# Loading the first 128 columns of x alone, in two halves, with w1 slabs between the other columns, in a dense SiLU kernel

## Chip, cores, metric

One core of one Trainium2 chip. The metric is device time in microseconds (us) for one execution, lower is better. Runs are compared against the kernel before in the same rounds on the same chip.

## The reference

```python
B, S, D, F = 1, 2048, 640, 1728        # all bf16
h   = silu(einsum("bsd,df->bsf", x, w1))
out = einsum("bsf,fd->bsd", h, w2)
```

The kernel's matmuls contract over partitions, so x is needed transposed, with D on partitions. x is worked on in four chunks of 512 rows. Chunks 1 to 3 come through transposing DMAs, hidden behind the first chunk's matmuls. Chunk 0 is wanted at once: it is loaded plainly and transposed on TensorE by matmuls with an identity.

## The kernel before

The parts that matter are the opening loads and TensorE's opening. `FB` is 512, `KF` 4, `TPC` 4, `TA` 2, `DT` 5.

```python
# SyncE
load_x(0)                   # x rows 0-127, all 640 columns, 160 KB
load_slab(0)                # w1 rows 0-127, first 512 columns, 128 KB
for j in range(2, TPC):
    load_x(j)
for d in range(3, DT):
    load_slab(d)
for g, (a, b) in enumerate(G_COLS):         # the rest of w1: G0 480 KB, G1 1040 KB
    sp.dma_start(out=w1_sb[:, :, a:b], in_=w1_v[:, :, a:b]).then_inc(sem_w1g[g], 16)
...
# ScalarE, before its table load
act.dma_start(out=x_sb[:, 1, :], in_=xf[P:2 * P, :]).then_inc(sem_xb[1], 16)
for d in range(1, 3):
    act.dma_start(out=w1_sb[:, d, 0:FB], in_=w1_v[:, d, 0:FB]).then_inc(sem_w1[d], 16)
...
# TensorE
busy(W_FIRST)               # 12 + 15 dummy matmuls to raise the clock
need(sem_id, 2)
busy(W_SECOND)
transpose(0)                # five 128x128 transposes of row block 0, ready for two copies
transpose(1)
for j in range(2):
    for d in range(TA):
        early(d, j, j + 1)  # 4 matmuls: w1 slab d, rows of block j
transpose(2)
early(2, 0, 2)
for d in range(3):
    early(d, 2, 3)
transpose(3)
early(3, 0, 3)
for d in range(4):
    early(d, 3, 4)
early(4, 0, 4)
# then the main loop: 240 matmuls of 512 columns (L310 before, L330 after)
```

ScalarE copies the transposes of slabs 0 and 1 out of PSUM, VectorE those of slabs 2 to 4.

Of the kernel before, what the change touches and what calls it, by code (L numbers as in the profile page):

```python
# [8 lines left out]
def bass_standalone__dense_activation_silu__prompt_kernel(  # L9
# [9 lines left out]
    xf = x.flatten_outer_dims()  # L19
# [3 lines left out]
    P = 128  # L23
# [14 lines left out]
    TA = 2  # L38
    W_FIRST, W_SECOND = 12, 15
    assert TPC == 4 and FB + FQ < F and TA * P <= CH and (DT - TA) * P <= CH  # L40

# [59 lines left out]
    with ExitStack() as es:  # L101
# [19 lines left out]
        sem_xb = [sem(f"sem_xb{j}") for j in range(TPC)]  # L121
# [16 lines left out]

        w1_v = w1.rearrange("(d p) f -> p d f", p=P)
        w2_v = w2[0:NF * P, :].rearrange("(f p) d -> p f d", p=P)  # L140
        ones = nc.const_aps.tensor(1.0, [P, CH], bf16)

# [13 lines left out]
        def on_sync(sp):  # L156
            def load_x(j):
                sp.dma_start(
                    out=x_sb[:, j, :], in_=xf[j * P:(j + 1) * P, :]
                ).then_inc(sem_xb[j], 16)  # L160
# [6 lines left out]
            load_x(0)  # L167
            load_slab(0)
            for j in range(2, TPC):
                load_x(j)  # L170
            for d in range(3, DT):
                load_slab(d)
# [42 lines left out]
        def on_tensor(pe):  # L215
# [17 lines left out]
            def transpose(j):  # L233
                need(sem_xb[j], 16)
                if j >= 2:
                    need(sem_cpa, j - 1)
                    need(sem_cpv, j - 1)
                ba = 4 + 2 * (j % 2)
                for d in range(DT):
                    k = d if d < TA else d - TA  # L240
                    ins = pe.matmul(  # L241
                        ps[:, ba + (d >= TA), k * P:(k + 1) * P],
                        lhsT=x_sb[:, j, d * P:(d + 1) * P],
                        rhs=ident[:, :],
                        start=True,
                        stop=True,
                    )
                    if d == TA - 1:
                        ins.then_inc(sem_tpa, 1)
                ins.then_inc(sem_tpv, 1)  # L250

            def early(d, j0, j1):
                need(sem_w1[d], 16)
                need(sem_cpa if d < TA else sem_cpv, j1)
                for f in range(KF):
                    ins = pe.matmul(  # L256
                        ps[:, f, j0 * P:j1 * P],
                        lhsT=w1_sb[:, d, f * P:(f + 1) * P],
                        rhs=xT[:, d, j0 * P:j1 * P],
                        start=(d == 0 and j0 == 0),  # L260
# [3 lines left out]
                    if d == DT - 1 and j1 == TPC:  # L264
                        ins.then_inc(sem_pe1, 1)
# [4 lines left out]
            transpose(0)  # L270
            transpose(1)
            for j in range(2):
                for d in range(TA):
                    early(d, j, j + 1)
            transpose(2)
            early(2, 0, 2)
            for d in range(3):
                early(d, 2, 3)
            transpose(3)
            early(3, 0, 3)  # L280
            for d in range(4):
                early(d, 3, 4)
            early(4, 0, 4)

            for i in range(KF, NU):
# [7 lines left out]
                if i < NB:  # L293
                    need(sem_cpa, TPC)
                    need(sem_cpv, TPC)
# [58 lines left out]
        def on_scalar(act):  # L354
            act.dma_start(
                out=x_sb[:, 1, :], in_=xf[P:2 * P, :]
            ).then_inc(sem_xb[1], 16)
            for d in range(1, 3):
                act.dma_start(
                    out=w1_sb[:, d, 0:FB], in_=w1_v[:, d, 0:FB]  # L360
                ).then_inc(sem_w1[d], 16)
# [3 lines left out]
            for j in range(TPC):  # L365
                act.wait_ge(sem_tpa, j + 1)
                act.copy(  # L367
                    out=xT[:, 0:TA, j * P:(j + 1) * P],
                    in_=ps[:, 4 + 2 * (j % 2), 0:TA * P].rearrange("p (d s) -> p d s", s=P),
# [19 lines left out]
        def on_vector(dve):  # L389
            for j in range(TPC):  # L390
                dve.wait_ge(sem_tpv, j + 1)
# [44 lines left out]
```

## Time and profile before

| | before |
|---|---|
| median of the first 3 runs | 126.31 us (126.29 to 127.24) |
| profiled execution | 126.98 us, span 125.7 us |
| PE busy | 122.9 us, 98% of the span |
| main loop (L310) starts | 10.40 us |

"Span" is the profile's first to last instruction, about 1.3 us shorter than the time. A line of the timeline gives start, length, engine, source line, operation, output<-input, shape and count, and in brackets idle time before it with what ended it. The profile's lines are in the prediction below.

### The profile page before, as it was taken

The numbers are of one execution on the slowest core, as the hardware profiler recorded it, in microseconds if no ns is written. First come the engines' busy times: TensorE is split into PE (matmuls) and PEld (weight loads), VectorE is DVE, ScalarE is ACT, GpSimd is POOL, SyncE is SP. The second block draws the span as 40 slices with busy tenths as digits, with TensorE's granted clock in tenths as the row PEclk, the third lists the DMA queues.
The fourth block names the chain that finished last, engine by engine and source line by source line (L and its number), as shares of the span: only waits on it lengthen the run. The fifth ranks groups of instructions, "written<-read, shape, count | busy, mean of one in ns | idle before, by whom it ended". The sixth has DMA issues, their size and how long they took to land.

```text
span 125.7 us, 1483 instructions
## 1 busy us (share of the span) xinstructions
PE 122.9 (98%) x657; PEld 59.6 (47%) x657; DVE 12.2 (10%) x20; ACT 37.1 (30%) x65; POOL 0.7 (1%) x6
## 2 busy tenths in 40 slices
PE   7999999999999999999999999999999999999994
PEld 7884444444444444444444444443444443444452
DVE  0330000000000000000000000000700003920421
ACT  3328555555555555555540000001500000000000
POOL 2000000000000000000000000000000000000000
DMA  3992999990000000000000000000346000731022
GB/s 101 357 390 80 218 204 203 310 390 28 0 0 0 0 3 0 0 0 5 0 0 0 0 0 0 0 0 5 75 92 219 0 0 0 258 110 54 0 104 94
DMA packets 17014, 10.37 MB, mean 82 GB/s; under 512 B 10736, under 2 KB 17008, under 8 KB 17008
## 3 DMA queue, kind: packets, MB, share of 16 engines
q1 hardware_dynamic: 16432, 9.82, 26.4%
q10 hardware_dynamic: 576, 0.46, 1.1%
q8 instruction: 5, 0.08, 0.3%
q14 instruction: 1, 0.01, 0.0%
HBM read 5.16 MB, written 2.62 MB: 62 GB/s over the span
## 4 chain that ended last, share of the span: by engine, by line
PE 95%; DMA 2%; ACT 0%; issue 0%
PE ps L344 47%; PE ps L310 41%; PE ps L256 4%; DMA x_sb<-in_x_dram 2%; PE ps L301 2%; PE ps L241 1%; ACT o_sb L381 0%
## 5 line engine op out<-in xcount | busy, mean ns | idle before, releaser
L310 PE MATMUL ps<-xT,w_sb 128*128 128x512 bf16 x240 | 52.0, 379 | 0.0
L344 PE MATMUL ps<-w_sb,hT 128*128 128x512 bf16 (+2 forms) x221 | 45.6, 367 | 0.0
L374 ACT ACTIVATE hT<-ps 128x512 bf16<-128x512 f32 x52 | 30.6, 598 | 24.0 <-PE ps L310 22.4
L310 PEld LDWEIGHTS ps<-xT,w_sb 128*128 128x128 bf16 x240 | 23.5, 98 | 28.3
L344 PEld LDWEIGHTS ps<-w_sb,hT 128*128 128x128 bf16 x221 | 20.9, 98 | 24.5 <-issue 0.6
L399 DVE CAST o_sb<-ps 128x512 bf16<-128x512 f32 (+1 forms) x16 | 10.0, 677 | 104.9 <-PE ps L344 104.9
L344 PE MATMUL ps<-hT,w_sb 128*128 128x512 bf16 x52 | 11.4, 379 | 0.0
L381 ACT CAST o_sb<-ps 128x128 bf16<-128x128 f32 x1 | 0.3, 266 | 34.2 <-PE ps L344 34.2
L381 ACT CAST oT<-ps 128x512 bf16<-128x512 f32 x4 | 2.1, 600 | 22.3 <-PE ps L344 22.3
L344 PEld LDWEIGHTS ps<-hT,w_sb 128*128 128x128 bf16 x52 | 5.0, 98 | 6.3 <-issue 0.4
L256 PE MATMUL ps<-xT,w_sb 128*128 128x128 bf16 (+3 forms) x56 | 5.4, 258 | 0.0
L256 PEld LDWEIGHTS ps<-xT,w_sb 128*128 128x128 bf16 x56 | 4.1, 108 | 0.7
L225 PE MATMUL ps<-const-bfloat16-1.0 128*128 128x128 bf16 x27 | 3.0, 312 | 0.8 <-PEq L421 0.8
L225 PEld LDWEIGHTS ps<-const-bfloat16-1.0 128*128 128x128 bf16 x27 | 2.8, 148 | 0.7 <-issue 0.7
L392 DVE CAST xT<-ps 128x384 bf16<-128x384 f32 x4 | 2.2, 558 | 6.5 <-PE ps L241 6.5
L367 ACT CAST xT<-ps 128x256 bf16<-128x256 f32 x4 | 1.5, 373 | 3.3 <-PE ps L241 3.3
L301 PE MATMUL ps<-xT,w_sb 128*64 128x512 bf16 x20 | 2.3, 381 | 0.0
L344 PE MATMUL ps<-w_sb,hTl 64*128 64x512 bf16 (+2 forms) x17 | 2.2, 366 | 0.0
L241 PE MATMUL ps<-ident,x_sb 128*128 128x128 bf16 x20 | 2.1, 265 | 0.1
L362 ACT ACT_TABLE_LOAD x1 | 1.3, 1283 | 2.2 <-issue 2.2
L241 PEld LDWEIGHTS ps<-ident,x_sb 128*128 128x128 bf16 x20 | 1.6, 120 | 0.3 <-DMA x_sb<-in_x_dram 0.3
L301 PEld LDWEIGHTS ps<-xT,w_sb 128*64 128x64 bf16 x20 | 1.0, 110 | 1.2 <-ACT hT L374 0.4
(11 smaller groups left out, 3.7 us busy)
## 6 DMA issues: line engine op xcount, KB each, us to landing
out_dram<-o_sb SPq DMA_DIRECT2D x15, 160.0 KB, 1.8
w_sb<-in_w_dram SPq DMA_DIRECT2D x1, 1120.0 KB, 7.6
w_sb<-in_w_dram SPq DMA_DIRECT2D x1, 1040.0 KB, 6.8
w_sb<-in_w_dram SPq DMA_DIRECT2D x1, 960.0 KB, 5.3
x_sb<-in_x_dram SPq DMA_DIRECT2D x3, 160.0 KB, 4.0
w_sb<-in_w_dram SPq DMA_DIRECT2D x1, 480.0 KB, 4.7
w_sb<-in_w_dram SPq DMA_DIRECT2D x3, 128.0 KB, 3.7
w_sb<-in_w_dram ACTq DMA_DIRECT2D x2, 128.0 KB, 3.8
```

The lines of the kernel that those rows point to most:

```text
L225: pe.matmul(ps[:, KF - 1, 0:P], lhsT=ones[:, 0:P], rhs=ones[:, 0:P], start=True, stop=True,)
L241: ins = pe.matmul(ps[:, ba + (d >= TA), k * P:(k + 1) * P], lhsT=x_sb[:, j, d * P:(d + 1) * P], rhs=ident[:, :], start=True, stop=True,)
L256: ins = pe.matmul(ps[:, f, j0 * P:j1 * P], lhsT=w1_sb[:, d, f * P:(f + 1) * P], rhs=xT[:, d, j0 * P:j1 * P], start=(d == 0 and j0 == 0), s ...
L301: ins = pe.matmul(ps[h * FL:(h + 1) * FL, b, :], lhsT=w1_sb[:, d, NF * P:F], rhs=xT[:, d, (c + h) * CH:(c + h + 1) * CH], start=(d == 0), ...
L310: ins = pe.matmul(ps[:, b, :], lhsT=w1_sb[:, d, f * P:(f + 1) * P], rhs=xT[:, d, c * CH:(c + 1) * CH], start=(d == 0), stop=(d == DT - 1),)
L344: ins = pe.matmul(ps[:, bank, 0:width], lhsT=w_op if kind == "T" else h_op, rhs=h_op if kind == "T" else w_op, start=(first2[key] == i), s ...
L362: act.activation(out=warm_sb[:, :], in_=nc.const_aps.tensor(0.0, [P, 1], fp32), func=ACT.Silu)
L367: act.copy(out=xT[:, 0:TA, j * P:(j + 1) * P], in_=ps[:, 4 + 2 * (j % 2), 0:TA * P].rearrange("p (d s) -> p d s", s=P),).then_inc(sem_cpa, 1)
L374: act.activation(out=dst, in_=ps[:, i % NB, :], func=ACT.Silu).then_inc(sem_act1, 1)
L381: act.copy(out=dst, in_=ps[:, place[key], 0:dst.shape[-1]]).then_inc(sem_evb, 1)
L392: dve.tensor_copy(out=xT[:, TA:DT, j * P:(j + 1) * P], in_=ps[:, 5 + 2 * (j % 2), 0:(DT - TA) * P].rearrange("p (d s) -> p d s", s=P),).th ...
L399: dve.tensor_copy(out=o_sb[:, key[1], cols], in_=ps[:, place[key], cols]).then_inc(sem_eva, 1)
```

## The change

The intent: let TensorE start its real work sooner. Instead of waiting for a whole row block of x (160 KB), it waits for two loads of 64 KB that hold only columns 0 to 127 of all 512 rows, enough for the first slab of w1. The other 512 columns follow in two halves of 256 rows, with the slabs of w1 between them, in the order of need. (A slab is 128 rows of w1, first 512 columns; G0 and G1 are the rest of w1.) The dummy matmuls go from 27 to 21. The copies of the transposes are cut anew as well: pieces of 128 or 256 columns, taken in turn by ScalarE and VectorE.

```diff
-    W_FIRST, W_SECOND = 12, 15
+    W_FIRST, W_SECOND = 12, 9
...
+            def load_half(k):
+                js = slice(k * JH, (k + 1) * JH)
                 sp.dma_start(
-                    out=x_sb[:, j, :], in_=xf[j * P:(j + 1) * P, :]
-                ).then_inc(sem_xb[j], 16)
+                    out=x_sb[:, js, P:D], in_=x_v[:, js, P:D]
+                ).then_inc(sem_xh[k], 16)
...
-            load_x(0)
+            sp.dma_start(
+                out=x_sb[:, 0:JH, 0:P], in_=x_v[:, 0:JH, 0:P]
+            ).then_inc(sem_xf[0], 16)
             load_slab(0)
-            for j in range(2, TPC):
-                load_x(j)
-            for d in range(3, DT):
-                load_slab(d)
+            load_half(0)
+            load_slab(1)
+            load_slab(2)
+            load_half(1)
+            load_slab(3)
+            load_slab(4)
...
             act.dma_start(
-                out=x_sb[:, 1, :], in_=xf[P:2 * P, :]
-            ).then_inc(sem_xb[1], 16)
-            for d in range(1, 3):
-                act.dma_start(
-                    out=w1_sb[:, d, 0:FB], in_=w1_v[:, d, 0:FB]
-                ).then_inc(sem_w1[d], 16)
+                out=x_sb[:, JH:TPC, 0:P], in_=x_v[:, JH:TPC, 0:P]
+            ).then_inc(sem_xf[1], 16)
...
+            for i in range(TPC):
+                transpose(i)                        # slab 0, all 512 rows
+            for j in range(TPC - 1):
+                early(0, j * P, (j + 1) * P)
+            transpose(at[1, 0]); transpose(at[2, 0])     # (joined here)
+            early(0, CH - P, CH)
+            transpose(at[3, 0]); transpose(at[4, 0])
+            early(1, 0, HC)
+            early(2, 0, HC, range(KF // 2))
+            transpose(at[1, HC]); transpose(at[2, HC])   # first use of the second half
+            early(2, 0, HC, range(KF // 2, KF))
+            transpose(at[3, HC]); transpose(at[4, HC])
+            early(1, HC, CH)
+            early(2, HC, CH)
+            early(3, 0, CH)
+            early(4, 0, CH)
```

More of the change, by code (lines that the diff above doesn't have):

```diff
@@ L37, in bass_standalone__dense_activation_silu__prompt_kernel @@
     TPC = CH // P
-    TA = 2
-    W_FIRST, W_SECOND = 12, 15
-    assert TPC == 4 and FB + FQ < F and TA * P <= CH and (DT - TA) * P <= CH
+    HC = CH // 2
+    JH = TPC // 2
+    W_FIRST, W_SECOND = 12, 9
+    assert TPC == 4 and FB + FQ < F and DT == 5
     units = [(c, f) for c in range(NC) for f in range(NF)]
@@ L120, in bass_standalone__dense_activation_silu__prompt_kernel @@
         sem_id = sem("sem_id")
-        sem_xb = [sem(f"sem_xb{j}") for j in range(TPC)]
+        sem_xf = [sem(f"sem_xf{k}") for k in range(2)]
+        sem_xh = [sem(f"sem_xh{k}") for k in range(2)]
         sem_tpa = sem("sem_tpa")
@@ L137, in bass_standalone__dense_activation_silu__prompt_kernel @@
         sem_ol = sem("sem_ol")
+        x_v = xf[0:CH, :].rearrange("(j p) d -> p j d", p=P)
         w1_v = w1.rearrange("(d p) f -> p d f", p=P)
@@ L141, in bass_standalone__dense_activation_silu__prompt_kernel @@
         ones = nc.const_aps.tensor(1.0, [P, CH], bf16)
+        turns = [(0, j * P, (j + 1) * P, KF + j) for j in range(TPC)]
+        for k in range(2):
+            turns += [(d, k * HC, (k + 1) * HC, KF + d - 1) for d in range(1, DT)]
+        at = {(d, a): i for i, (d, a, b, bank) in enumerate(turns)}
         def on_gpsimd(pool):
@@ L156, in on_sync @@
         def on_sync(sp):
-            def load_x(j):
+            def load_half(k):
+                js = slice(k * JH, (k + 1) * JH)
                 sp.dma_start(
-                    out=x_sb[:, j, :], in_=xf[j * P:(j + 1) * P, :]
-                ).then_inc(sem_xb[j], 16)
+                    out=x_sb[:, js, P:D], in_=x_v[:, js, P:D]
+                ).then_inc(sem_xh[k], 16)
             def load_slab(d):
@@ L231, in busy, with copied, transpose @@
                     )
-            def transpose(j):
-                need(sem_xb[j], 16)
-                if j >= 2:
-                    need(sem_cpa, j - 1)
-                    need(sem_cpv, j - 1)
-                ba = 4 + 2 * (j % 2)
-                for d in range(DT):
-                    k = d if d < TA else d - TA
+            def copied(i):
+                need(sem_cpv if i % 2 else sem_cpa, i // 2 + 1)
+            def transpose(i):
+                d, a, b, bank = turns[i]
+                need((sem_xh if d else sem_xf)[a // HC], 16)
+                if i >= TPC:
+                    copied(i - TPC)
+                for off in range(0, b - a, P):
                     ins = pe.matmul(
-                        ps[:, ba + (d >= TA), k * P:(k + 1) * P],
-                        lhsT=x_sb[:, j, d * P:(d + 1) * P],
+                        ps[:, bank, off:off + P],
+                        lhsT=x_sb[:, (a + off) // P, d * P:(d + 1) * P],
                         rhs=ident[:, :],
@@ L247, in transpose, with early @@
                     )
-                    if d == TA - 1:
-                        ins.then_inc(sem_tpa, 1)
-                ins.then_inc(sem_tpv, 1)
-            def early(d, j0, j1):
+                ins.then_inc(sem_tpv if i % 2 else sem_tpa, 1)
+            def early(d, a, b, fs=range(KF)):
                 need(sem_w1[d], 16)
-                need(sem_cpa if d < TA else sem_cpv, j1)
-                for f in range(KF):
+                step = HC if d else P
+                for c0 in range(a, b, step):
+                    copied(at[d, c0])
+                for f in fs:
                     ins = pe.matmul(
-                        ps[:, f, j0 * P:j1 * P],
+                        ps[:, f, a:b],
                         lhsT=w1_sb[:, d, f * P:(f + 1) * P],
-                        rhs=xT[:, d, j0 * P:j1 * P],
-                        start=(d == 0 and j0 == 0),
+                        rhs=xT[:, d, a:b],
+                        start=(d == 0 and a == 0),
                         stop=(d == DT - 1),
@@ L263, in early @@
                     )
-                    if d == DT - 1 and j1 == TPC:
+                    if d == DT - 1:
                         ins.then_inc(sem_pe1, 1)
@@ L269, in on_tensor @@
             busy(W_SECOND)
-            transpose(0)
-            transpose(1)
-            for j in range(2):
-                for d in range(TA):
-                    early(d, j, j + 1)
-            transpose(2)
-            early(2, 0, 2)
-            for d in range(3):
-                early(d, 2, 3)
-            transpose(3)
-            early(3, 0, 3)
-            for d in range(4):
-                early(d, 3, 4)
-            early(4, 0, 4)
+            for i in range(TPC):
+                transpose(i)
+            for j in range(TPC - 1):
+                early(0, j * P, (j + 1) * P)
+            transpose(at[1, 0])
+            transpose(at[2, 0])
+            early(0, CH - P, CH)
+            transpose(at[3, 0])
+            transpose(at[4, 0])
+            early(1, 0, HC)
+            early(2, 0, HC, range(KF // 2))
+            transpose(at[1, HC])
+            transpose(at[2, HC])
+            early(2, 0, HC, range(KF // 2, KF))
+            transpose(at[3, HC])
+            transpose(at[4, HC])
+            early(1, HC, CH)
+            early(2, HC, CH)
+            early(3, 0, CH)
+            early(4, 0, CH)
             for i in range(KF, NU):
@@ L293, in on_tensor @@
                 if i < NB:
-                    need(sem_cpa, TPC)
-                    need(sem_cpv, TPC)
+                    copied(len(turns) - 2)
+                    copied(len(turns) - 1)
                 else:
@@ L364, in on_scalar @@
             )
-            for j in range(TPC):
-                act.wait_ge(sem_tpa, j + 1)
+            for n, (d, a, b, bank) in enumerate(turns[0::2]):
+                act.wait_ge(sem_tpa, n + 1)
                 act.copy(
-                    out=xT[:, 0:TA, j * P:(j + 1) * P],
-                    in_=ps[:, 4 + 2 * (j % 2), 0:TA * P].rearrange("p (d s) -> p d s", s=P),
+                    out=xT[:, d, a:b], in_=ps[:, bank, 0:b - a]
                 ).then_inc(sem_cpa, 1)
@@ L389, in on_vector @@
         def on_vector(dve):
-            for j in range(TPC):
-                dve.wait_ge(sem_tpv, j + 1)
+            for n, (d, a, b, bank) in enumerate(turns[1::2]):
+                dve.wait_ge(sem_tpv, n + 1)
                 dve.tensor_copy(
-                    out=xT[:, TA:DT, j * P:(j + 1) * P],
-                    in_=ps[:, 5 + 2 * (j % 2), 0:(DT - TA) * P].rearrange("p (d s) -> p d s", s=P),
+                    out=xT[:, d, a:b], in_=ps[:, bank, 0:b - a]
                 ).then_inc(sem_cpv, 1)
```

## The prediction

> **What bounds the kernel now.** I read the page's chain first, then the timeline from 3 to 11 us, then the waits, then stretches of half a microsecond for the DMA.
>
> The chain that ended last (us from the start, us long, what):
>
> ```profile
> PE 95%; DMA 2%; ACT 0%; issue 0%
> ...
> 0.74 3.09 DMA x_sb<-in_x_dram
> 3.83 0.05 issue
> 3.88 1.25 PE ps L241 x10
> 5.12 1.33 PE ps L256 x16
> 6.46 0.28 PE ps L241 x5
> 6.74 1.14 PE ps L256 x16
> 7.88 0.28 PE ps L241 x5
> 8.16 2.41 PE ps L256 x24
> 10.56 51.80 PE ps L310 x240
> ```
>
> One DMA, the first 128 rows of x, holds TensorE until 3.88; from there TensorE alone carries the program to its end. 240 matmuls of L310 in 51.80 us are 215.8 ns each for 512 columns. The change touches nothing behind L310's first matmul, so its whole worth is how much earlier that matmul starts. The timeline has it at 10.40 (the chain counts ends of pipelined matmuls, so it says 10.56).
>
> The timeline of the opening, PE and copies (start, us, what):
>
> ```profile
> 0.78 3.04 PE L225 MATMUL ps<-const-bfloat16-1.0 128*128 128x128 bf16 x27 [0.78 <-PEq L421]
> ...
> 3.87 0.99 PEld L241 LDWEIGHTS ps<-ident,x_sb 128*128 128x128 bf16 x10 [0.32 <-DMA x_sb<-in_x_dram]
> 3.88 1.25 PE L241 MATMUL ps<-ident,x_sb 128*128 128x128 bf16 x10
> 4.31 0.37 ACT L367 CAST xT<-ps 128x256 bf16<-128x256 f32 x1 [0.65 <-PE ps L241]
> ...
> 4.92 1.54 PE L256 MATMUL ps<-xT,w_sb 128*128 128x128 bf16 x16
> 6.24 0.32 PEld L241 LDWEIGHTS ps<-ident,x_sb 128*128 128x128 bf16 x5
> 6.30 0.44 PE L241 MATMUL ps<-ident,x_sb 128*128 128x128 bf16 x5
> ...
> 6.58 1.30 PE L256 MATMUL ps<-xT,w_sb 128*128 128x256 bf16 x16
> ```
>
> Three things are to be seen. The 27 dummy matmuls are over just before x comes. From 3.88 no PE or PEld line carries a wait for data, so the old order of transposes and early matmuls already hides every later load. And TensorE changes speed: ten transposes take 4.92 - 3.88 = 1.04 us (104 ns each), the next five 6.58 - 6.30 = 0.28 us (56 ns each). The sixteen L256 matmuls between take 6.30 - 4.92 = 1.38 us; with n of them at 107 and the rest at 56 ns, n is 9.5, so the switch lies near 5.9 us. The PEclk column says 1.00 throughout and hides it.
>
> **The opening as a sum.** 20 transposes of 128 columns, and 44 x 128 + 4 x (256 + 384 + 512) columns of L256, are 12,800 columns in 76 matmuls. At full speed 12,800 / 2.4 = 5.33 us; the 20 or so matmuls before 5.9 are 2,560 columns at half speed, 1.07 us more; 56 fast matmuls at 2.5 ns overhead are 0.14. The sum is 6.54 us; the timeline has 10.40 - 3.88 = 6.52. So there is no bubble in it to remove, and the 128-column matmuls cost nothing special.
>
> **What the Trainium skill says.** "TensorE: Matmul & The Clock Gate", section "Back-to-back issue gap": N / 1.2 ns cold and N / 2.4 + 2.5 ns warm, 107 and 56 ns for 128 columns. The trace agrees (104 and 56). The same page, "What's actually happening": the clock is released after a busy window of about 3.4 us, and the window is free-running. One trace cannot show whether it runs free, but 5.9 is 5.1 us after the first dummy matmul, which would fit one partly filled window and then a full one. "DMA: Bandwidth & Descriptors", section "Issuing engines are not separate DMA queues": loads from both queues share the same 16 engines. The trace agrees as far as it goes: the total stays between 329 and 409 GB/s from 2.5 to 9.5 us, with two queues in use or one. Its "Specifications" give 512 B as the least transfer for line rate. The new first loads move rows of 256 B; nothing in this trace's opening does, so their cost is not shown here.
>
> **Part 1, the first loads.** Before, TensorE waits for 160 KB beside 160 KB from the other queue. After, two loads of 64 KB stand first. From the stretches (the last column is GB/s):
>
> ```profile
> 1.50:2.00 0.50, 0.50 (x7) 0.50 (x6) 0.00 (x0) 0.00 (x0) 0.00 (x0) 1.00 0.50 61
> 2.00:2.50 0.50, 0.50 (x8) 0.50 (x6) 0.00 (x0) 0.34 (x1) 0.00 (x0) 1.00 0.70 131
> 2.50:3.00 0.50, 0.50 (x8) 0.50 (x6) 0.00 (x0) 0.50 (x1) 0.00 (x0) 1.00 0.94 329
> 3.00:3.50 0.50, 0.50 (x7) 0.50 (x6) 0.00 (x0) 0.49 (x2) 0.00 (x0) 1.00 1.08 380
> ```
>
> 30, 65, 165 and 190 KB arrive in these halves: 95 by 2.5, 260 by 3.0, 450 by 3.5. The two old x loads, 320 KB, are through by about 3.16; the queue views have them landed at 0.74 + 3.1 = 3.83 and 0.74 + 3.3 = 4.05, so 0.7 to 0.9 us later. The same lag on 128 KB (through by 2.6) gives 3.3 to 3.5. The short rows may eat a little, a smaller load may be told sooner; the author's cut from 27 to 21 dummies ends them near 0.84 + 20 x 0.107 + 0.1 = 3.1, which suggests 3.1 to 3.3 was aimed at. I take a start at 3.35, half a microsecond earlier.
>
> **Part 2, the later loads.** By the same byte curve and lag I place slab 0 (256 KB in all) at 3.8, the first half of the other columns (512) at 4.5, slabs 1 and 2 at 4.9 and 5.3, the second half (1,024) at 6.1, slabs 3 and 4 at 6.4 and 6.8, the next weight group at about 8. All issue from one queue at 0.47 us each (the old one's spacing), the last of these eight at about 4.0: well ahead of their landing, so issuing does not bind.
>
> **Part 3, TensorE's new order.** The columns are the same 12,800: 20 x 128 of transposes, then 16 x 128 + 16 x 256 + 8 x 512. 60 matmuls instead of 76 save 16 x 2.5 ns = 0.04 us. What is new is a thin start: only four transposes (3.35 to about 3.75) before the first matmul that needs a copy. A copy began 0.35 us after the start of the slow matmul it waited for (3.96 to 4.31); ScalarE takes 0.27 us for 128x128 (row L381). So 3.35 + 0.35 + 0.27 + 0.07 (my guess for the signal) = 4.04: a bubble of 0.3 us. Then twelve matmuls to 5.32, four transposes to 5.75, and part of the next group until the clock rises at 5.9. Slow columns done by then: 4 x 128 + (5.90 - 4.04) x 1,200 = 2,744, against 2,560 before. The rest, 10,056 columns, is 4.19 us plus 0.1 of overhead: 10.19, or **0.21 us** earlier.
>
> The half microsecond of start shrinks to this because the bubble eats 0.3 of it, and because what is gained before 5.9 is gained at half speed.
>
> Against it one wait: the transpose of the second half's slab 1 is issued near 6.92; its second matmul at 6.98 plus 0.26 (6.35 to 6.61 in the trace) starts ScalarE's 0.37 us copy, ready at 7.68 with the signal, where TensorE would be at about 7.58. **0.1 us** back. The copies split evenly otherwise, and the old ones of 0.56 us on VectorE become ones of some 0.3 and 0.4. The page's ScalarE and VectorE are idle enough here. Sum: 10.40 - 0.21 + 0.10 = 10.29, some 0.1 us saved. If x lands at 3.2 instead, another 0.07.
>
> **Rivals.** *A load takes over as the wait.* The last halves and slabs stand in one queue; if the 256 B rows slow the first loads by 0.5 us, everything behind moves too. But the margins are wide: the second half is due at 6.1 and wanted at 6.9, slab 3 at 6.4 and wanted near 8.5. Only x's first half and slab 0 have none; 0.5 us there costs 0.25 us net: 126.5. *The clock rises later.* Two gaps, 3.1 to 3.35 and 3.75 to 4.04, against one of 0.3 now, fall into the stretch before 5.9. If that is too idle and the rise comes one window (3.4 us) later, the cold time costs 3.4 / 2 = 1.7 us: 128. For it: 0.5 to 0.6 us idle in a window where 0.3 passed. Against: TensorE still works over 80% of it. I give it one in ten. *No bubble, all the gain.* If the copies come sooner than I think, 0.5 us of early start gives 0.25 plus 0.04: about 126.0. *The clock rises earlier* has no reason in the change.
>
> **Range and chances.** The time before is 126.31, with one run of three at 127.24, so single runs move by nearly 1 us by themselves. I predict 126.2 and take 125.6 to 127.0: the lower end holds the full gain and some luck, the upper a late load or a median from the slower kind of run. A change of 2% needs 2.5 us. The whole wait for x is 3.1 us and most of it stays, so faster by that is all but excluded (0.01). Slower needs the late clock and more besides, 1.7 not being enough (0.02). Within 2%: 0.97.
>
> **What would show it.** Right: the first transpose at 3.2 to 3.4; a PE or PEld idle of about 0.3 us before the first L-line of early matmuls, put down to a ScalarE copy; cadence from 107 to 56 ns near 5.9; no DMA wait on TensorE after slab 0; L310's successor starting at 10.2 to 10.4; everything behind it the same length. Wrong: a first transpose not before 3.7 (small rows), or TensorE waiting for a slab or a half, or the change of cadence at another time, which would outweigh all the rest: every microsecond by which it moves is half a microsecond of the total.

## The result

127.43 us median (127.31 to 127.58, 6 runs) against 126.58 (126.29 to 127.24, 6 runs). The ratio is 1.0061, interval [1.0033, 1.009]. A ratio is the mean time of one kernel's runs over that of the other's in the same rounds, so not quite the ratio of the medians. Executions over 1.5% slower than the fastest of the same kernel are left out of the means. So the change is 0.6% slower: within 2%, as given most of the chance, but above the range of 125.6 to 127.0 and in the other direction than the small gain that was foretold. 0.3 us of the miss on the absolute number is the baseline, whose median rose from 126.31 to 126.58 with three more runs.

The chain that ended last, after the change (start, us, what):

```profile
0.74 0.45 SPq L176
...
2.74 0.43 SPq L172
3.17 0.04 issue
3.22 4.26 DMA x_sb<-in_x_dram
7.48 0.05 issue
7.53 0.40 PE ps L255 x4
...
11.05 51.80 PE ps L330 x240
```

Before, the chain left the DMAs at 3.83 us and stayed on TensorE. Now it leaves them at 7.48: SyncE's issues one after another, then a load issued at 3.22 that takes 4.26 us to land. It is the second half of x. L330's 51.80 us are those of L310 to the hundredth, so nothing behind it has changed.

The timeline of TensorE's opening after the change:

```profile
3.03 0.61 PE L255 MATMUL ps<-ident,x_sb 128*128 128x128 bf16 x4
3.35 0.48 ACT L383 CAST xT<-ps 128x128 bf16<-128x128 f32 x2 [0.61 <-PE ps L255]
...
3.73 1.20 PEld L270 LDWEIGHTS ps<-xT,w_sb 128*128 128x128 bf16 x12 [0.36 <-DMA w_sb<-in_w_dram]
3.76 1.44 PE L270 MATMUL ps<-xT,w_sb 128*128 128x128 bf16 x12
...
6.28 0.91 PE L270 MATMUL ps<-xT,w_sb 128*128 128x256 bf16 x6
...
7.52 0.23 PEld L255 LDWEIGHTS ps<-ident,x_sb 128*128 128x128 bf16 x4 [0.62 <-DMA x_sb<-in_x_dram]
...
10.89 2.32 PE L330 MATMUL ps<-xT,w_sb 128*128 128x512 bf16 x10
```

The first transpose is at 3.03, sooner than hoped. There is the small bubble before 3.76. But then TensorE stands idle until 7.52 for the second half, and the main loop starts at 10.89 instead of 10.40: 0.49 us, which is the spans' difference (126.14 - 125.66). The rise of the clock, from half speed to full, is read from the distance of starts: of the six matmuls from 6.28 the first takes 0.196 us to the next, the others 0.109, and at half speed it would be 0.21. So some (0.196 - 0.109) x 2 = 0.17 us of it were at half speed, and the clock rose near 6.45, not at 5.9. (The same working gives 5.93 for the kernel before.)

Landings of the opening loads, us from the start (issue plus time to landing, per load):

| | before | after | before, second trace | after, second trace |
|---|---|---|---|---|
| first x | 3.83 and 4.03 | 2.98 and 3.17 | 3.45 and 3.68 | 2.97 and 3.16 |
| slab 0 | 4.33 | 3.60 | 4.04 | 3.47 |
| slab 1, slab 2 | 4.56, 5.87 | 5.29, 6.40 | 4.26, 6.39 | 5.41, 6.71 |
| rest of x | 5.64 and 6.10 | 4.96 and 7.48 | 6.18 and 6.70 | 5.07 and 7.49 |
| slab 3, slab 4 | 6.46, 6.79 | 7.85, 8.93 | 7.05, 7.39 | 7.83, 8.16 |
| G0, G1 | 8.24, 10.89 | 10.28, 12.89 | 8.67, 11.67 | 10.60, 13.24 |

(The second traces were taken later, see the experiments.)

The bytes are the same, but after the first x and slab 0 nearly everything is late, in the end by 2 us (against the second trace before, by less). Where it is lost can be read from half-microsecond stretches. The columns are the busy time and count of PE, PEld, DVE, ACT and POOL, then granted clock, busy share of the DMA engines and GB/s. Before:

```profile
4.50:5.00 0.50, 0.50 (x7) 0.50 (x6) 0.37 (x1) 0.34 (x2) 0.00 (x0) 1.00 1.03 330
5.00:5.50 0.50, 0.50 (x8) 0.50 (x6) 0.50 (x2) 0.21 (x1) 0.00 (x0) 1.00 1.06 361
5.50:6.00 0.50, 0.50 (x8) 0.50 (x6) 0.22 (x1) 0.00 (x0) 0.00 (x0) 1.00 1.09 378
```

After:

```profile
4.50:5.00 0.50, 0.50 (x7) 0.44 (x5) 0.00 (x0) 0.00 (x0) 0.00 (x0) 1.00 0.79 182
5.00:5.50 0.50, 0.50 (x7) 0.49 (x6) 0.00 (x0) 0.05 (x1) 0.00 (x0) 1.00 0.71 152
5.50:6.00 0.50, 0.50 (x8) 0.50 (x6) 0.33 (x1) 0.33 (x1) 0.00 (x0) 1.00 0.65 184
```

Half the rate, with the DMA engines idle for a fifth to a third of the time, although eight loads on SyncE's queue had been issued by 4.6 us. Another dip, of 133 GB/s, lies at 3.0 to 3.5. The second trace of the kernel before has a dip of its own, shallower and shorter (233 and 255 GB/s from 4 to 5 us, then 359 and 369), for which nothing waits; that after has 268, 115 and 166 in the three stretches. Single packets, the pieces in which a DMA engine moves a load, go the same way, but less clearly: of those read between 2.5 and 9 us, 48 and 45 took over 130 ns ("long" below) in the two traces after (up to 1,260 ns), 13 and 24 in the two before (up to 1,540 ns). The usual packet of 1,024 B takes 46 ns in both.

### The profile page after: what moved, and what is told of

It is laid out like the page before. It is cut to its first block, busy times and chain, and to the rows that moved or that the text cites. A ratio compares the mean times of both kernels' runs of the same rounds, so it can differ in the third digit from the quotient of the medians.

```text
span 126.1 us, 1445 instructions
## 1 busy us (share of the span) xinstructions
PE 123.0 (98%) x635; PEld 58.9 (47%) x635; DVE 12.2 (10%) x22; ACT 37.6 (30%) x67; POOL 0.7 (1%) x6
## 4 chain that ended last, share of the span: by engine, by line
PE 93%; DMA 3%; SPq 2%; issue 0%; ACT 0%
PE ps L364 47%; PE ps L330 41%; DMA x_sb<-in_x_dram 3%; PE ps L270 2%; PE ps L321 2%; SPq L172 1%; PE ps L255 0%; SPq L176 0%; SPq L167 0%; ACT o_sb L396 0%
## 5 line engine op out<-in xcount | busy, mean ns | idle before, releaser
L330 PE MATMUL ps<-xT,w_sb 128*128 128x512 bf16 x240 | 52.0, 379 | 0.0
L330 PEld LDWEIGHTS ps<-xT,w_sb 128*128 128x128 bf16 x240 | 23.5, 98 | 28.3
L270 PE MATMUL ps<-xT,w_sb 128*128 128x128 bf16 (+2 forms) x40 | 6.1, 312 | 0.1
L238 PE MATMUL ps<-const-bfloat16-1.0 128*128 128x128 bf16 x21 | 2.4, 309 | 0.8 <-PEq L435 0.8
L383 ACT CAST xT<-ps 128x256 bf16<-128x256 f32 (+1 forms) x6 | 2.0, 337 | 3.9 <-PE ps L255 3.9
L255 PE MATMUL ps<-ident,x_sb 128*128 128x128 bf16 x20 | 2.6, 274 | 0.3 <-DMA x_sb<-in_x_dram 0.3
L407 DVE CAST xT<-ps 128x256 bf16<-128x256 f32 (+1 forms) x6 | 2.2, 380 | 6.6 <-PE ps L255 6.6
L238 PEld LDWEIGHTS ps<-const-bfloat16-1.0 128*128 128x128 bf16 x21 | 2.2, 143 | 0.7 <-issue 0.7
```

Of the source, the lines that this page charges most:

```text
L238: pe.matmul(ps[:, KF - 1, 0:P], lhsT=ones[:, 0:P], rhs=ones[:, 0:P], start=True, stop=True,)
L255: ins = pe.matmul(ps[:, bank, off:off + P], lhsT=x_sb[:, (a + off) // P, d * P:(d + 1) * P], rhs=ident[:, :], start=True, stop=True,)
L270: ins = pe.matmul(ps[:, f, a:b], lhsT=w1_sb[:, d, f * P:(f + 1) * P], rhs=xT[:, d, a:b], start=(d == 0 and a == 0), stop=(d == DT - 1), sk ...
L330: ins = pe.matmul(ps[:, b, :], lhsT=w1_sb[:, d, f * P:(f + 1) * P], rhs=xT[:, d, c * CH:(c + 1) * CH], start=(d == 0), stop=(d == DT - 1),)
L383: act.copy(out=xT[:, d, a:b], in_=ps[:, bank, 0:b - a]).then_inc(sem_cpa, 1)
L407: dve.tensor_copy(out=xT[:, d, a:b], in_=ps[:, bank, 0:b - a]).then_inc(sem_cpv, 1)
```

## The experiments

Theories at the start: the **one queue** (all loads but one now issue from SyncE), the **form** of the new loads (pieces of 1,024 B out of rows of 1,280, two row blocks per load), and the mere **place** of the second half in the line. Variants of the changed kernel first, run on one chip (kernel before there: 126.88 median).

**Row blocks.**

```diff
-                sp.dma_start(
-                    out=x_sb[:, js, P:D], in_=x_v[:, js, P:D]
-                ).then_inc(sem_xh[k], 16)
+                for j in range(k * JH, (k + 1) * JH):
+                    sp.dma_start(
+                        out=x_sb[:, j, P:D], in_=x_v[:, j, P:D]
+                    ).then_inc(sem_xh[k], 16)
```

> The changed kernel, but each half of x's other columns comes as two loads of 128 rows instead of one load of 256 (two row blocks per partition); 2 more DMAs on SyncE's queue, each some 0.47 us of issue. In the changed kernel the second half lands at 7.48 us and TensorE starts L330 at 10.89. If the two-block form of the load is what makes it slow: second half at 6.5 or before, the wait of 0.51 us gone, 126.9 us or less. If the one queue is at fault (fewer loads in flight at once): no better, the second half at 7.5 or later (two more loads), 127.4 to 127.8 us. If only its place in the queue: 7.5, 127.4.

Measured: 127.28 us (126.83 to 127.7), ratio 1.0047 [1.0013, 1.008]. The second half landed at 6.77 and TensorE no longer waited for it. That alone would speak for the form. But the slow stretches had only moved: 180 GB/s at 4.5 to 5.0, 295 and 307 up to 6.0, and then 164 and 202 from 6.5 to 7.5, G0 landed at 10.19 (10.28 in the changed kernel), and L330 waited for it. Neither forecast held (6.5 and 126.9 for the form, 7.5 and 127.4 to 127.8 for the queue): a mixed verdict, against the number of loads in its simplest reading too, as two more loads did not make the whole slower.

**Whole rows.**

```diff
-                    out=x_sb[:, js, P:D], in_=x_v[:, js, P:D]
+                    out=x_full[:, js, :], in_=x_v[:, js, :]
...
-                        lhsT=x_sb[:, (a + off) // P, d * P:(d + 1) * P],
+                        lhsT=(x_full if d else x_sb)[:, (a + off) // P, d * P:(d + 1) * P],
```

> The changed kernel, but the halves are loaded as whole rows of 1280 B (all 640 columns, into a buffer of their own), so that what is read in DRAM is contiguous again; a quarter more bytes in them. If the pieces of 1024 B out of 1280 B rows stall the DMA engines: the long packets (over 130 ns) from 3.0 to 5.6 us become few as before, the second half lands at 6.6 or sooner in spite of 128 KB more, 127.0 us or less. If the single queue or the place in it is at fault: at 7.5 to 7.9, 127.4 to 127.7 us.

Measured: 127.78 us (127.74 to 127.99), ratio 1.0078. 49 long packets, the second half at 7.75: late with whole rows too, so the broken rows are not needed for it. That they add nothing is not shown. The stretches from 4.5 to 6 us were less low here (319, 228 and 281 GB/s), slab 0 came late instead (4.71), and TensorE waited 1.2 us for it, which is part of the time.

**Two queues.**

```diff
             load_half(0)
-            load_slab(1)
-            load_slab(2)
             load_half(1)
...
+            for d in range(1, 3):            # on ScalarE's queue
+                act.dma_start(
+                    out=w1_sb[:, d, 0:FB], in_=w1_v[:, d, 0:FB]
+                ).then_inc(sem_w1[d], 16)
```

> The changed kernel, but slabs 1 and 2 are issued from ScalarE's queue right after its first load of x, as the kernel before does; order on SyncE's queue otherwise as it is. If one queue alone is what starves the DMA engines (they moved 150 to 180 GB/s from 4.5 to 6 us where the kernel before had 330 to 378): that stretch is back over 300 GB/s, the second half lands at 6.3 or sooner, the wait of 0.51 us is gone and the time is 126.4 to 126.9 us. If the form of the halves' loads is at fault: bytes stay slow, the second half at 7 or later, 127.2 us or more. Both can be told apart by the GB/s from 4.5 to 6.

The stretches of this variant:

```profile
4.50:5.00 0.50, 0.50 (x8) 0.50 (x6) 0.00 (x0) 0.00 (x0) 0.00 (x0) 1.00 0.95 320
5.00:5.50 0.50, 0.46 (x5) 0.24 (x3) 0.00 (x0) 0.00 (x0) 0.00 (x0) 1.00 1.07 361
5.50:6.00 0.50, 0.30 (x6) 0.30 (x7) 0.00 (x0) 0.00 (x0) 0.00 (x0) 1.00 1.10 365
```

The rate is that of the kernel before, long packets are down to 24, the second half lands at 6.22 and G0 at 8.26. So moving two loads cures the rate, with the form of the halves as it was. The time was not cured: 128.01 us median (127.04 to 129.15), two of four runs near 127.1 and two near 129 (one of them counted slow, its span 127.8). In the trace, of a good run, the first half now lands at 5.66 instead of 4.96, as slabs 1 and 2 now come beside it, and TensorE idles twice, 3.4 to 4.07 and 5.3 to 5.70. The first gap ends with ScalarE's first copy, not with a load: two issues more on ScalarE put its table load off from 1.25 to 2.27 us and that copy from 3.35 to 3.67. The expected 126.4 to 126.9 was missed. The bad runs were not traced; what they may be came out later.

**Half first.**

```diff
             load_half(0)
+            load_half(1)
             load_slab(1)
             load_slab(2)
-            load_half(1)
```

> The changed kernel with the second half of x ahead of slabs 1 and 2 in the queue. If only its place in the queue is at fault: the half lands some 0.9 us sooner (6.5), slabs 1 and 2 0.9 later (6.2 and 7.2), and as slab 1 is wanted at 6.28 and slab 2 at about 6.7, the wait moves to slab 2 and shrinks a little: 127.2 us. If a low rate of bytes is the cause, whoever stands third in line waits: about the same time, 127.2 to 127.6 us, with TensorE waiting for w1 instead of x.

Measured: 127.3 us (126.99 to 127.35), ratio 1.0032 [1.0006, 1.0058]. The second half at 5.66, slabs 1 and 2 at 6.06 and 6.79, and TensorE waits three times for w1, 1.0 us in all on its weight loads. Whoever stands third in the line waits, as the low rate would have it; another place cures nothing by itself. Whether it helps a little is open (the interval overlaps the changed kernel's).

**The old kernel on one queue**, on another chip (kernel before there: 127.14 median). This asks whether one queue slows the old loads as well.

```diff
             load_x(0)
+            load_x(1)
-            load_slab(0)
+            for d in range(3):
+                load_slab(d)
...
-            act.dma_start(out=x_sb[:, 1, :], ...)
-            for d in range(1, 3):
-                act.dma_start(out=w1_sb[:, d, 0:FB], ...)
```

> The kernel before with its nine first loads all issued by SyncE, in about the order of their issue before (x0, x1, slabs 0 to 2, x2, x3, slabs 3 and 4); shapes of the loads and TensorE's order untouched. If one queue alone lowers the rate, whatever the shape of the loads: under 250 GB/s in some of the stretches from 3 to 6.5 us where the kernel before had 330 to 378, many long packets, slab 4 landing after 7.5 instead of 6.79, TensorE waiting for w1 or x for some 0.3 to 1 us, 127.2 us or more. If it takes the new shapes (256 B rows, two-block halves) as well: the rate stays over 320 from 3.5 us on, slab 4 before 7.3, 126.3 to 127.1 us.

Its stretches:

```profile
4.50:5.00 0.50, 0.50 (x8) 0.47 (x6) 0.50 (x2) 0.37 (x1) 0.00 (x0) 1.00 0.92 305
5.00:5.50 0.50, 0.50 (x9) 0.44 (x8) 0.47 (x1) 0.00 (x0) 0.00 (x0) 1.00 0.84 214
5.50:6.00 0.50, 0.50 (x10) 0.34 (x7) 0.00 (x0) 0.00 (x0) 0.00 (x0) 1.00 0.66 161
```

127.38 us (127.36 to 127.75), ratio 1.0045 [1.0002, 1.0087]; 53 long packets; slab 4 at 7.85; TensorE waits 0.6 us for x. All marks set for one queue were met (under 250 GB/s, slab 4 after 7.5, a wait of 0.3 to 1 us, 127.2 us or more). None of the change's new shapes is in this kernel, and it shows the changed kernel's dip.

**Both kernels once more**, for second traces.

> The kernel before, unchanged, for a second trace. Theory: the clock's rise comes at another moment in each execution (5.9 us in the first trace, 5.2 to 6.3 in the traces of the variants), and the kernel before, which waits for no load after the first, follows it by half: with the rise at another time t, L310 starts near 10.40 - (5.93 - t) / 2. Rival: the rise is fixed by the kernel's own matmuls, then it lies at 5.9 again and the spread of the times comes from elsewhere.

The kernel before: the clock rose near 6.04, L310 started at 10.34, the dummies ended at 3.61 and x had landed at 3.45, 0.4 us sooner than in the first trace. Half of the 0.27 us earlier start less half of the 0.11 later rise is 0.08 us, against 0.06 found. So the rise and the start of work both count by half, but the rise had hardly moved: that it wanders between executions of this kernel is not shown, and the forecast from the rise alone, 10.46, missed. What did differ between the two traces is the loads (table and dip above).

> The changed kernel, unchanged, for a second trace. Theory: its opening is set by the landing of the second half of x, not by the clock, which is why its six times lie within 0.27 us where those of the kernel before spread over 0.95. So with the rise of the clock elsewhere than 6.3 us, the second half lands at 7.3 to 7.6 again and L330 starts at 10.7 to 11.0 all the same, the wait for the half being longer when the clock rises sooner. Rival (the late rise of 6.33 in the first trace made the time): a rise at 5.3 would bring L330 to 10.4.

The changed kernel: second half at 7.49, L330 at 10.89, both as in the first trace. The rise was at 6.45, as in the first, so this run did not tell the two theories apart as meant. The times do so better: seven runs of the changed kernel lie within 0.27 us, while most variants that do not wait for the second half spread by 0.7 to 2.1 us (half first, which waits for w1 instead, by 0.36).

**Halves on ScalarE's queue**, the same chip.

```diff
-            load_half(0)  ... load_slab(4)
+            for d in range(1, DT):
+                load_slab(d)
...
+            for k in range(2):               # on ScalarE's queue
+                js = slice(k * JH, (k + 1) * JH)
+                act.dma_start(
+                    out=x_sb[:, js, P:D], in_=x_v[:, js, P:D]
+                ).then_inc(sem_xh[k], 16)
```

> The changed kernel with both halves of x issued from ScalarE's queue and all slabs from SyncE's: two queues again, the first half earlier than in the two-queue variant before (landing 5.66 there). By equal shares: slab 0 at 3.9, first half and slab 1 at 4.7, slab 2 at 5.3, second half and slab 3 at 6.3, slab 4 at 6.7. If the rate of the queues is what set the changed kernel's time: no wait for a load but that for slab 0, L330 at 10.1 to 10.3 with the clock's rise at 5.9 and sooner when it rises sooner, 126.3 to 126.8 us, level with or a little under the kernel before on the same chip. If the two-block halves are slow by themselves: the second half after 7, 127.2 us or more. Some executions may miss a window of the clock, TensorE idling some 0.5 us before slab 0, and come out 1.7 us longer.

The loads were cured (363 to 383 GB/s from 4.5 to 6, second half at 6.33) except for slab 0, which landed at 4.68. The time, forecast at 126.3 to 126.8, was by far the worst: 128.76 us (128.38 to 129.06), ratio 1.0142. Its timeline says why:

```profile
4.72 1.46 PE L260 MATMUL ps<-xT,w_sb 128*128 128x128 bf16 x12 [1.13 <-DMA w_sb<-in_w_dram]
...
7.26 1.49 PE L260 MATMUL ps<-xT,w_sb 128*128 128x256 bf16 x6
...
9.39 0.44 PE L245 MATMUL ps<-ident,x_sb 128*128 128x128 bf16 x4
...
12.27 1.03 PE L320 MATMUL ps<-xT,w_sb 128*128 128x512 bf16 x4
```

The six matmuls from 7.26 take 0.21 us each, half speed. The rise comes only at 9.5, 3.3 us later than in the next variant (6.2), about the window of 3.4 us that the prediction took from the Trainium skill ("TensorE: Matmul & The Clock Gate", "What's actually happening"). This is the prediction's second rival. Only one run was traced; the other three times lie close to its 128.85.

**The same with eleven dummy matmuls in the idle time**, and three more, on a third chip (kernel before there: 126.86 median).

```diff
             for i in range(TPC):
                 transpose(i)
+            busy(11)
```

> The variant with both halves on ScalarE's queue (its clock rose only at 9.5 us, after TensorE had idled from 3.4 to 4.7 for slab 0; 128.76 us) with eleven dummy matmuls put into that idle time. All loads and real instructions are the same. If the idle time is what made the clock miss its window: rise at 6.4 or before, L320 at 10.5 to 11.0 instead of 12.27, 126.9 to 127.4 us. If the late rise came from something else: no change, 128.4 to 129 us.

```profile
3.42 1.38 PE L228 MATMUL ps<-const-bfloat16-1.0 128*128 128x128 bf16 x11
...
6.16 0.43 PE L245 MATMUL ps<-ident,x_sb 128*128 128x128 bf16 x4
...
7.03 0.82 PE L260 MATMUL ps<-xT,w_sb 128*128 128x256 bf16 x6
...
11.03 2.32 PE L321 MATMUL ps<-xT,w_sb 128*128 128x512 bf16 x10
```

127.39 us (126.88 to 127.61), ratio 1.0033. Slab 0 was as late as without them (4.86), but the clock rose at 6.2 and the main loop started at 11.03 instead of 12.27. Idle time in the opening thus costs more than itself: work that computes nothing won 1.2 us. This also fits the two bad runs of the two-queue variant, though those were not traced.

**Fewer, larger loads on the one queue.**

```diff
-            load_half(0)  ... load_slab(4)
+            sp.dma_start(
+                out=x_sb[:, :, P:D], in_=x_v[:, :, P:D]
+            ).then_inc(sem_xh[0], 16)
+            for d in (1, 3):
+                sp.dma_start(
+                    out=w1_sb[:, d:d + 2, 0:FB], in_=w1_v[:, d:d + 2, 0:FB]
+                ).then_inc(sem_w1[d], 16)
```

> The changed kernel on its one queue, but with fewer and larger loads after slab 0: both halves of x as one load (512 KB), slabs 1 and 2 as one, slabs 3 and 4 as one (256 KB each). What in the one queue is slow? If it is the number of loads behind each other (each load's end holds the queue up): the stretches from 4.5 to 6.5 us come back over 300 GB/s and the long packets fall from 45 to 30 or less. If it is one queue's reads as such, whatever their grouping: 150 to 250 GB/s in some stretches and 45 or more long packets again. The time says little here, as the coarse loads land late for TensorE: x's other columns at 5.5 to 6, 127 to 128 us.

```profile
4.50:5.00 0.50, 0.27 (x5) 0.09 (x2) 0.00 (x0) 0.00 (x0) 0.00 (x0) 1.00 1.07 379
5.00:5.50 0.50, 0.00 (x0) 0.00 (x0) 0.00 (x0) 0.00 (x0) 0.00 (x0) 1.00 1.10 377
5.50:6.00 0.50, 0.00 (x0) 0.00 (x0) 0.00 (x0) 0.00 (x0) 0.00 (x0) 1.00 1.13 369
```

Still one queue, and the full rate. G0 landed at 8.78. The long packets fell to 34, between the two marks (30 or fewer, 45 or more). The dip from 3 to 4 us stayed (121 and 129 GB/s), where the first x, slab 0 and the large load still follow each other. The time, 127.86 us (127.46 to 129.69, the last counted slow, at a granted clock of 0.987), ratio 1.0066, goes with the coarse load of x, for which TensorE waited 1.3 us, as expected. So it is not one queue as such, but many small loads one behind another in it.

**No wait for the second half** (wrong result).

```diff
-                need((sem_xh if d else sem_xf)[a // HC], 16)
+                need(sem_xh[0] if d else sem_xf[a // HC], 16)
...
-                        lhsT=x_sb[:, (a + off) // P, d * P:(d + 1) * P],
+                        lhsT=x_sb[:, (a + off) // P % (JH if d else TPC), d * P:(d + 1) * P],
```

> The changed kernel with all loads as they are, but the transposes of the second half's columns 128 to 639 read the first half once more, so that nothing waits for the second half of x: a wrong result on purpose, to price that one wait. In the changed kernel the wait is 0.51 to 0.6 us and sets the end. Theory: L330 starts at 10.3 to 10.4 with the clock's rise at 6.3 to 6.4 (and sooner with a sooner rise), 126.8 to 127.0 us, spread again as before. Rival (another load, slab 3 or 4, landing at 7.85 and 8.2 to 8.9, takes its place): wait for w1 and 127.2 us or more.

```profile
10.69 2.55 PE L330 MATMUL ps<-xT,w_sb 128*128 128x512 bf16 x11 [0.21 <-DMA w_sb<-in_w_dram]
```

127.08 us (126.72 to 128.22), ratio 1.003 [0.9983, 1.0077]. Without that wait L330 could have gone at 10.32; it waited until 10.69 for G0, which landed at 10.65. Of 0.57 us that this wait would be worth by the clock of this trace (10.89 - 10.32), 0.2 were kept. The rival was right in kind, with G0 in the place of slab 3 or 4: the lateness is that of the whole line. (The median lies between the two forecasts, 127.0 or less and 127.2 or more.) And the times spread again, by 1.5 us.

**First half split over both queues, four dummies** (a try at beating both).

```diff
-            load_half(0)
-            load_slab(1)
+            sp.dma_start(out=x_sb[:, 1, P:D], ...).then_inc(sem_xh[0], 16)
             load_slab(2)
...
+            act.dma_start(out=x_sb[:, 0, P:D], ...).then_inc(sem_xh[0], 16)
+            act.dma_start(out=w1_sb[:, 1, 0:FB], ...).then_inc(sem_w1[1], 16)
...
+            busy(4)
```

> An attempt at a version better than both: the changed kernel on two queues, with the first half of x split by row blocks over both so that it does not fall behind: SyncE has first columns, slab 0, block 1, slab 2, second half, slabs 3 and 4; ScalarE has first columns, block 0, slab 1. Four dummy matmuls fill the idle time after the first four transposes. If the two queues cure the loads: slab 0 at 3.9, first half by 5.0, second half by 6.6, L330 near 10.25 at a rise of 5.9, against 10.4 of the kernel before: 126.5 to 127.0 us, 0 to 0.2 us under the kernel before in the same rounds. If slabs and halves, alone on SyncE's queue after 4.2 us, fall back into the slow rate: a wait of 0.3 us or more for the second half and 127.2 us or more.

127.33 us (126.87 to 128.81), ratio 1.0046 [1.0003, 1.0088]. A miss. Four of six runs lie from 126.87 to 127.49 and two at 128.7 and 128.8 (the latter counted slow); the traced one, 128.72, is of the bad ones. In it slab 0 landed at 5.06, TensorE idled from 3.8 to 5.1 in spite of four dummies, and the clock rose only at 8.65.

**The changed order with two loads fewer**, on the first of these chips again (kernel before: 126.77 median).

```diff
-            load_slab(1)
-            load_slab(2)
+            load_slabs(1)           # slabs 1 and 2 in one load
             load_half(1)
-            load_slab(3)
-            load_slab(4)
+            load_slabs(3)           # slabs 3 and 4 in one load
```

> The changed kernel, its order and its one queue kept, but slabs 1 and 2 in one load of 256 KB, and slabs 3 and 4 in one: two loads fewer after slab 0, and PE's order untouched. If the number of loads in the one queue is what cost the half microsecond: bytes back over 300 GB/s from about 4.5 us, first half at 5.0 as before, slabs 1 and 2 at 5.9, second half at 6.5, slabs 3 and 4 at 7.3, the next group at 8.8; no wait but that for slab 0 (0.35 us); L330 at 10.2 to 10.4 with the clock's rise near 6.3, so level with the kernel before, 126.6 to 127.0 us, and spreading with the clock again. If the halves of 256 KB count for as much as the slabs: second half after 7.0, wait of 0.2 us or more, 127.2 us or more.

```profile
6.30 1.08 PE L273 MATMUL ps<-xT,w_sb 128*128 128x256 bf16 x6
7.21 0.39 PE L258 MATMUL ps<-ident,x_sb 128*128 128x128 bf16 x4
...
10.56 2.75 PE L333 MATMUL ps<-xT,w_sb 128*128 128x512 bf16 x12
```

127.1 us (126.62 to 127.95), ratio 1.0029 [0.9996, 1.0062]. 295 to 348 GB/s from 4.5 to 6.5 us, second half at 6.39, G0 at 9.17, and no bracket before 7.21: the wait for x is gone. The clock rose late in this trace, near 6.82 (the first two of the six matmuls from 6.30 take 0.21 us each, the third 0.16), and that explains the 10.56: the prediction's 10.29, less 0.16 for the earlier start, plus 0.02 for the bubble, plus half of 6.82 - 5.93, less 0.02 for the copy, is 10.58. Without a wait for a load the prediction's sum holds. The long packets, 42, hardly fell. The spread is back as well, and the median misses the forecast of 126.6 to 127.0 by 0.1. It is the best of the correct variants, but no better than the kernel before, and its interval does not set it clearly apart from the changed kernel's.

Over all traces, the number of loads that stand in SyncE's queue ahead of G0 goes with the landing of G0, up to eight loads (same bytes in all but whole rows, which has 64 KB more in each half):

| loads ahead of G0 in SyncE's queue | kernels | G0 lands, us |
|---|---|---|
| 5 | fewer loads | 8.78 |
| 6 | before (twice), two queues, halves on ScalarE, the same with dummies, two loads fewer | 8.24, 8.67, 8.26, 8.78, 9.07, 9.17 |
| 7 | first half split | 9.62 |
| 8 | after (twice), whole rows, half first, no wait | 10.28, 10.60, 10.32, 10.19, 10.65 |
| 9 | old kernel on one queue | 9.63 |
| 10 | row blocks | 10.19 |

Beyond eight the number no longer orders them, and a load more is also an issue more. G0 was issued at 3.28 us with five loads ahead of it, at 3.5 to 3.8 with six, at 4.67 with eight and at 5.53 with ten; from there it took 4.6 to 6.0 us in all traces, without growing steadily (5.5 with five, 4.7 with nine and ten). So a good part of this table may be the later issue alone; no run separates the two for G0. For the second half the record does: in the row-blocks variant its last block was issued at 4.11, 0.9 us later than the half in the changed kernel, and landed at 6.77, 0.7 us sooner.

## Why the prediction was wrong, point by point

**Bound and worth: right.** L330 and all behind it kept their length, and the span moved by the start of the main loop (0.48 and 0.49 us).

**The first loads: right in kind, too cautious.** 3.03 instead of 3.35, worth half of 0.32. The short rows are slower byte for byte, as the prediction feared: their packets of 256 B took 18 ns, those of 1,024 B 46 ns, which is 14 against 22 bytes per ns. The loads still landed first. In the old kernel on one queue, though, the 160 KB of the first row block, with no second x load beside them, landed at 2.99 as well.

**The later loads: the step that failed.** The prediction used the old kernel's curve of bytes over time for a queue filled in another way: "so issuing does not bind". It put the second half at 6.1 and slabs 3 and 4 at 6.4 and 6.8; they landed at 7.48, 7.85 and 8.93. The curve was that of one trace, and of six loads in one queue and three in the other. The second trace of the same kernel had another: there the first 1,024 KB, for which the prediction read 6.1, had landed at 6.70, with 0.2 us left before the 6.9 at which the half was wanted. The old kernel's loads on one queue lose the rate (161 GB/s at worst), two queues restore it, and so do fewer loads on one queue. Slow issuing does not explain the half: in the changed kernel the time from issue to landing grows from 2.2 us for the first load to 4.3 for the half and 4.7 for slab 4, so the loads stood in line, and a block issued later landed sooner (row blocks). It is part of what came last: slabs 3 and 4 and G0 were issued 1.1 us later than before. What in the line costs the time, and why its place wanders (row blocks), stays open.

**The rival dismissed.** "A load takes over as the wait" was set aside because of margins of 0.8 and 2 us, margins taken from the same curve. It is what happened. The run without the wait for the half shows that it is the line as a whole: the next load, G0, took over.

**The bubble: right.** 0.33 us for 0.3. The profile's bracket puts it down to slab 0, but slab 0 landed at 3.60 and 3.47 in the two traces, and TensorE went on at 3.76 and 3.75. ScalarE's first copy, 0.27 us long from 3.35 and 3.34, ended 0.14 us before that in both: it was the copy, as foretold.

**The clock: taken as fixed.** 5.93 and 6.04 in the two traces before, 6.45 twice after, 5.48 and 5.34 in variants (row blocks, half first) whose TensorE program is the same, 6.82 in another (two loads fewer). One trace could not give that, and the late rise costs here half of 0.52 us. What sets the moment stays open. The rival of a missed window, given one in ten, did not occur in the changed kernel's traces. A rise about one window late stands in those of two variants (9.5 and 8.65), and the times of a third suggest it.

The sum, in the prediction's own terms for the traced run: 10.29, less 0.16 for the earlier start, plus 0.02 for the bubble, plus 0.26 for the rise, less 0.02 for the copy (0.08 for 0.10), plus 0.51 for the second half, is 10.90; the trace has 10.89. The wait for the half, foretold as zero, is the largest term. Run by run the loss is larger than between these two traces (127.44 - 126.67 = 0.77 us between the means), because the traced run of the kernel before, 126.98, was one of its slower ones. That would fit a kernel that gains when its clock rises soon, against one that then waits longer for a load. That the spread of the old kernel's times comes from the clock is argued from this and from the spread of the variants, not shown: its two traces have nearly the same rise.

## What to carry to other kernels

A curve of bytes over time belongs to the queues, the load sizes and the one execution that made it: when loads move to another queue or are cut smaller, place the later ones anew, and distrust margins read from the old curve. Starting TensorE earlier is worth half while its clock is low, and an idle gap put into that time can cost much more than itself (a rise 3.3 us later for 1.3 us idle here); dummy matmuls that fill the gap are cheap insurance. Eleven filled it here, four were too few in the split variant. A load moved to ScalarE's queue also delays what ScalarE has to do. Where time depends on such a moment, one trace of the kernel before is one draw: take more.

## What the Trainium skill lacked or had wrong

- "DMA: Bandwidth & Descriptors", "Rules for kernel authors" and "Issuing engines are not separate DMA queues": spreading loads over the issuing engines is said not to help bandwidth and to save issue time only. Here, with loads of 64 to 256 KB, moving two of them to the second queue took the stretch from 4.5 to 6 us from 152-184 (115-268 in the second trace) to 320-365 GB/s, and putting all of the old kernel's loads on one queue took it from 330-378 (255-369) down to 161-305. The issue time is called usually small there; here one issue takes 0.43 to 0.48 us, and 128 KB at 361 GB/s take 0.36. How much of the gain is issue time is not separated.
- The same page's rule to coalesce small loads agrees, but it gives no cost for loads that follow each other in one queue: joining six loads to three on one queue brought 369 to 379 GB/s from 4.5 to 6 us.
- The same page, "Specifications", is borne out, not wrong: it has 512 B as the least transfer for line rate, and here packets of 256 B moved 14 bytes per ns (18 ns each), those of 1,024 B 22 (46 ns).
- "TensorE: Matmul & The Clock Gate", "What's actually happening": nothing on how much idle time a window may hold before the first rise. 0.33 us was borne; with 1.3 us the rise came at 9.5 us in one kernel, 3.3 us later than with the gap filled, and not late in another (whole rows, idle from 3.4 to 4.76, at full speed from 4.8).
- No page speaks of the profile's column of granted clock (PEclk), which does not show this rise: it stands at 1.00 while matmuls of 128 columns follow each other at 107 ns.
